# Long convolution with a gated projection on one core: the third stage multiplies with its constants held still, block by block, and its results turn through DRAM

## The chip, the cores and the metric

The kernel runs on one core of a Trainium2 chip. The metric is the device time of one execution in microseconds (us). The engines are named as the profile names them: PE (TensorE, the matmuls), PEld (PE's weight loads), DVE (VectorE), ACT (ScalarE), POOL (GpSimd) and SP (SyncE, which issues every DMA of this kernel, in order).

## The reference

Eight sequences of 6400 steps and 128 channels, all in fp32. First a causal convolution of each channel with a filter as long as the sequence, then a short gated layer:

```python
B, S, D = x.shape                      # 8, 6400, 128;  h is (6400, 128)
L = 2 * S
y = np.fft.irfft(np.fft.rfft(x, n=L, axis=1) * np.fft.rfft(h, n=L, axis=0)[None], n=L, axis=1)[:, :S, :]
...
gate_pre[t] = sum over k of conv_w[k] * y[t - 4 + k]      # 5 taps, per channel
gate = 1.0 / (1.0 + np.exp(-gate_pre))
val = y @ w_val
out = gate * val @ w_out
```

## The kernel before

The transform of 6400 points is split into 100 x 64 (`N1`, `N2`), each part a matmul with a table of constants. For one sequence ("batch") there are four stages and a gated tail:

- **Stage 1** (`first_stage`), 16 groups of 8 channels. Four matmuls a group, the data as the stationary operand (100 x 128), the table `r1` moving (200 columns). ACT or DVE copies the result in four pieces of 64x400 into `gy`, which holds one whole batch with the channel outermost: `[128, 64 channel pairs, 100 k1, 2]`.
- **Stage 2** (`second`), 13 blocks `kb` of 8 values of k1 (the last has 4). Per k1 a matmul of 128 columns with a table from `m2`, loaded per block (512 KB). `product` multiplies the block by the filter's spectrum: `swap` (ACT, two copies of 64x1024 that exchange the halves), `times_re` and `times_im` (DVE), and `summed` (POOL, for the last two blocks also DVE), which leaves the result in `gy`. The filter's two tables (`hd`, in DRAM) are loaded by `h_load` for every block, twice 512 KB, since DRAM holds each of them on all 128 rows; some were stored as one half and doubled by DRAM-to-DRAM copies (`double`).
- **Stage 3** (line 753 on), 32 groups of 4 channels. Per channel one matmul: the channel's 100 values of k1 out of `gy` are the stationary operand (128 x 100), the table `r3` moves (128 columns). So the result has k1 on the partitions, where stage 4 needs it. ACT or DVE copies each group (100x512) into `dt`. It begins when all 13 products of the batch are there, and it frees `gy`, group by group, for stage 1 of the next batch.
- **Stage 4** (line 869 on), 13 chunks of 5 time columns (the head chunk has 4). Per column two matmuls of 100 columns with `m4`, the data out of `dt` stationary.
- **The tail** of each chunk: `yc` copies it out of PSUM, the taps are added up by ACT (`first`, `q`), DVE (`more`) and POOL (`third`); then the sigmoid (ACT), the first projection ("V" below, 500 columns with `w_val`), the gate (DVE), the second projection ("P" below, 500 columns with `w_out`), a copy and the store. From the eighth chunk on (`LAGGED`) the taps of a batch wait until the next batch's stage 3.

Ahead of all that lies the head: stages 1 and 2 of the filter `h` (`spectrum` keeps its tables and stores them to `hd`) beside stages 1 and 2 of the first batch, whose product is formed straight out of PSUM (`direct`).

The order of every engine's instructions is written by a planner (`_Plan`): each step has a cost per engine and a due time from constants such as `PERIOD`, and the planner runs them forward once, choosing engine, PSUM bank and buffer. The engines then follow that order, each strictly in sequence. Stage 2 works in two of PSUM's two-bank tiles (`ps`), everything else after the head in four banks (`pb`). Line 109, which the profile shows for nearly everything, is the helper that records an instruction.

Of the kernel before, what the change touches and what calls it, by code (L numbers as in the profile page):

```python
# [16 lines left out]
C = 128  # L17
# [16 lines left out]
LATE = 35  # L34
LAGGED = 8
WHOLE = 5
STASH = 6
M2B = 4
SLOTS = 11
# [3 lines left out]
HEAD_END = 101000  # L43
PERIOD = 126600
THIRD = 44275
FOURTH = 4511
SECOND = 3959
GATE = 13466
LAGS = 9341
EARLY = 545  # L50
# [5 lines left out]
LAST = 3177  # L56
LAST_GATE = 12434
# [66 lines left out]
class _Bank:  # L124


    def __init__(self, n, wide=False):
        self.n, self.wide, self.place = n, wide, None
# [5 lines left out]
class _Slot:  # L134


    def __init__(self, head=False):
        self.users, self.head, self.place = [], head, None
# [18 lines left out]
class _Plan:  # L157
# [63 lines left out]
    def forward(self):  # L221
# [4 lines left out]
        slots = [0] * (SLOTS + 2)  # L226
        self.split = False
        port = server = now = 0
        events, began = [], []
# [11 lines left out]
        def open_slots(o):  # L241
            n = len(slots) if o.take.head else SLOTS
            return [i for i in range(n) if slots[i] is not None and slots[i] <= now]
# [19 lines left out]
        while left:  # L263
            moved = True
            while moved:
                moved = False
                for e in free:
# [20 lines left out]
                    if e == "sync":  # L288
                        server = max(now + self.LEAD, server) + dur
                        free[e] = max(free[e], server - self.LEAD - self.AHEAD)  # L290
                        o.done = server + self.LAND
                    else:
                        o.done = now + dur + self.HOP
                    if o.port and e in ("vector", "gpsimd"):
                        port = now + dur
                    if o.take is not None:
                        i = o.take.spot = min(open_slots(o), key=lambda i: (i < SLOTS, slots[i]))
                        slots[i] = None
# [6 lines left out]
                    if b is not None:  # L305
                        if o.new:
                            i, h = b.spot = self.room(b, halves, now)
                            self.split = self.split or b.n == 1 and i > 1
                            for k in (0, 1) if b.n == 2 or i < 2 else (h,):
                                halves[i][k] = None  # L310
# [40 lines left out]
    def room(self, b, halves, now):  # L351
# [3 lines left out]
        if b.n == 2:  # L355
            return next(((i, 0) for i, p in enumerate(free) if all(p) and (i < 2 or not self.split)), None)
        spot = None
        if self.split or all(all(p) for p in free[2:]):
            spot = next(((i, h) for i in (2, 3) for h in (0, 1) if free[i][h]), None)
# [33 lines left out]
def longconv_moe(ctx: ExitStack, tc: tile.TileContext, x, h, r1, m2, r3, m4, w64, out):  # L393
# [9 lines left out]
    dt = cp.tile([128, N2 * 2 * C], F32, name="dt")  # L403
    dv = dt.rearrange("p (n c d) -> p n c d", c=2, d=C)
    gh = dt[:, : N1 * C].rearrange("p (d k t) -> p d k t", k=N1, t=2)
    m4_all = cp.tile([128, N2 + 1, N1], F32, name="m4_sb")
    m4_sb = m4_all[:PX]
# [4 lines left out]
    gl = cp.tile([128, N2 - LATE, N1], F32, name="gl")  # L412
    y_sb = [cp.tile([128, XG * N2], F32, name=f"y_{i}") for i in range(YB)]
# [19 lines left out]
    def kdt(t, kb):  # L433
        n = count(kb)
        return t[:, : n * C].rearrange("p (d k t) -> p d k t", k=n, t=2)

    def spectral(bank, kb):
        n = count(kb)
        if n <= 4:
            return bank.ap()[:, 0, : n * C].rearrange("p (k d t) -> p d k t", t=2, d=C // 2)  # L440
        return bank.ap().rearrange("p b (k d t) -> p d (b k) t", t=2, d=C // 2)
# [7 lines left out]
    def cells(y, n):  # L449
        out, i = [], 0  # L450
        while i < n:
            z = y + i
            end = 4 if z < 4 else LATE if z < LATE else N2
            k = min(n - i, end - z)
            s = (z - 4) % N2
            out.append((i, gl[:, z - LATE : z - LATE + k] if z >= LATE else dv[:, s : s + k, 1, :N1]))
            i += k
        return out

    def weights():
        ti = gl.rearrange("p n t -> p (n t)")[:, : 3 * NW].bitcast(I32)
        tf = gl.rearrange("p n t -> p (n t)")[:, 3 * NW : 6 * NW]
# [43 lines left out]
        last = dma(ti[:, : 2 * NW], w64.bitcast(I32), 261)  # L508
# [74 lines left out]
    def m2_load(kb):  # L583
        k, slot, n = count(kb), _Slot(), len(m2_user)
        rows = lambda: slot.ap().rearrange("p (k c) -> p k c", c=C)[:, :k]
        op = dma(rows, m2[:, kb * KB : kb * KB + k], 64 * k, m2_user[n - M2B] if n >= M2B else [], 6000, take=slot, spare=1)
# [20 lines left out]
    def summed(kb, w, u, after, many):  # L607
# [3 lines left out]
        if kb >= NKB - many:  # L611
            where["vector"] = _dve(count(kb) * C)
        return add(
            lambda e: getattr(nc, e).tensor_tensor(out=u, in0=u, in1=kdt(w.ap(), kb), op=ADD),
            where, after, port=True, use=[w],
        )

    def times_re(kb, p, bank, hs, u, after):
        return add(
            lambda e: nc.vector.tensor_tensor(out=u, in0=spectral(bank, kb), in1=kdt(hs[0].ap(), kb), op=MUL),  # L620
            {"vector": _dve(count(kb) * C)}, [p, *after], bank=bank, use=hs[:1],
        )

    def direct(kb, p, bank, hs, re, im):
        n, w = count(kb) * C, _Slot(True)
        u = gy[:, :, kb * KB : kb * KB + count(kb)]

        def cross(e):
            t, v, hi = kdt(w.ap(), kb), spectral(bank, kb), kdt(hs[1].ap(), kb)
# [3 lines left out]
        a = times_re(kb, p, bank, hs, u, re)  # L633
        c = _times(_dve(n, held=True), 2)
        b = add(cross, {"vector": (c[0] + 120, c[1] + 30)}, [p, *im], bank=bank, take=w, use=hs[1:])
        return a, b, summed(kb, w, u, [a, b], 1)

    def product(kb, p, bank, hs, h_ready):
        n, w = count(kb) * C, _Slot()
        u = gy[:, :, kb * KB : kb * KB + count(kb)]  # L640

        def swap(e):
            t, v = kdt(w.ap(), kb), spectral(bank, kb)
            nc.scalar.activation(t[:N2], v[N2:], AF.Copy, scale=1.0 if kb < WHOLE else -1.0)
            nc.scalar.copy(t[N2:], v[:N2])

        def times_im(e):
            t = kdt(w.ap(), kb)
            nc.vector.tensor_tensor(out=t, in0=t, in1=kdt(hs[1].ap(), kb), op=MUL)
# [3 lines left out]
        a = times_re(kb, p, bank, hs, u, h_ready[:1])  # L653
        b = add(times_im, {"vector": _dve(n)}, [s, h_ready[1]], port=True, use=[hs[1], w])
        return summed(kb, w, u, [a, b], MANY)

    def h_load(kb):
        k, hs = count(kb) * C, [_Slot(), _Slot()]
# [20 lines left out]
    w_in = weights()  # L679
    stored, head_done, adds = [], [], []  # L680

    def spectrum(kb, load):
        bank, n, hs = _Bank(2), count(kb) * C, [_Slot(True), _Slot(True)]
        v = lambda: spectral(bank, kb)
        t = lambda r: kdt(hs[r].ap(), kb)
# [3 lines left out]
        r1_ = add(  # L689
            lambda e: nc.gpsimd.tensor_copy(hs[0].ap()[N2:, :n], hs[0].ap()[:N2, :n]),  # L690
            {"gpsimd": (170 + 0.86 * n,) * 2}, [r0], use=hs[:1],
        )
        i0 = add(lambda e: nc.scalar.activation(t(1)[:N2], v()[N2:], AF.Copy, scale=-1.0), cost, [p], bank=bank, take=hs[1])
        i1 = add(lambda e: nc.scalar.copy(t(1)[N2:], v()[N2:]), cost, [p], bank=bank, use=hs[1:])
        full = kb < WHOLE
        m = 2 * N2 if full else N2
        st = [dma(hd[kb, 0, :m, :n], lambda: hs[0].ap()[:m, :n], n // (2 if full else 4), [r0, *([r1_] if full else [])], use=hs[:1])]
        lo = 0 if full else N2
        st.append(dma(
            hd[kb, 1, lo:, :n], lambda: hs[1].ap()[lo:, :n], n // (2 if full else 4), [i1, *([i0] if full else [])], use=hs[1:],  # L700
        ))
        stored.append([[x] for x in st])
        return p, hs, [r0, r1_], [i0, i1], st

    for kb in range(NKB):
        plan.where = f'head {kb}'
        plan.base = 46300 + 3680 * kb
# [3 lines left out]
        plan.base += 2760  # L711
        q = second(gy, kb, stat, xs1, bank)
        a, b, c = direct(kb, q, bank, hs, re, im)
        head_done += [p, a, b, *st]
        adds.append(c)

    stashed = first_stage(x[1], stash_at, lambda g: [*firsts[: 2 * NG]], HEAD_END - 1000, 1350, range(STASH)) if B > 1 else []
# [9 lines left out]
    def double(kb, after):  # L727
        n = count(kb) * C
        lo, hi = slice(0, N2), slice(N2, 2 * N2)
        for r, (o, i) in enumerate(((hi, lo), (lo, hi))):  # L730
            stored[kb][r] = [dma(hd[kb, r, o, :n], hd[kb, r, i, :n], n // 4, [*stored[kb][r], *after])]

# [8 lines left out]
    gl_user = {}  # L741
    s4_old, dt_old, tail_old = [], head_done, {}
# [3 lines left out]

    for b in range(B):
# [308 lines left out]
```

## Time and profile before

| | before |
|---|---|
| median of 3 runs | 1047.68 us (1047.63 to 1047.81) |
| the profiled execution | 1047.48 us |
| its span, first to last instruction | 1045.7 us |
| granted clock of TensorE | 1.000 |
| moved by DMA | 221.16 MB, mean 211 GB/s |
| read from and written to DRAM | 184.47 MB and 39.32 MB |

The profile gives the busy time of each engine, the chain of work that ended last, groups of instructions with their mean duration, and the DMA issues. A matmul in fp32 stands in the trace as two records, so a count of 16 is 8 matmuls. A record's duration contains the way through the array, which the next record overlaps; what a matmul costs in a row of them is the distance from start to start.

### The profile page before, as it was taken

To read this page: it belongs to the slowest core of one execution; us is meant where nothing else is said; L and a number is where in the kernel's file an instruction comes from. 1 tells how busy PE (TensorE), PEld (TensorE's weight loads), DVE (VectorE), ACT (ScalarE), POOL (GpSimd) and SP (SyncE) were. 2 spreads that over 40 slices of the span, in tenths; PEclk is the share of its full clock that TensorE was granted. 3 is DMA by queue.
4 is the path that set the end of the run, shared out by engine and by line. 5 is a ranking of instruction groups with operands and counts; after the bars stand their busy time and mean duration, and the time that the engine had idled before them with its cause. 6 is when DMAs were issued, how large, how long until landed. Compare 5 with 4: busy or idle time off the path is not lost.

```text
span 1045.7 us, 19783 instructions
## 1 busy us (share of the span) xinstructions
PE 1037.2 (99%) x7490; PEld 937.5 (90%) x7490; DVE 752.1 (72%) x1033; ACT 794.1 (76%) x1322; POOL 347.7 (33%) x229
## 2 busy tenths in 40 slices
PE   9999999999999999999999999999999999999998
PEld 9998999889988899888998899988998889988885
DVE  6999248983699637985399745996369953898187
ACT  6688679766886869777697767878688786987675
POOL 0078106610165203731056300652027410472030
PEclk9999999999999999999999999999999999999999
DMA  9598949953399335983289633994249931691102
GB/s 267 164 351 291 357 115 327 367 195 90 118 369 365 105 92 204 370 296 91 81 287 357 230 91 90 354 356 161 87 156 377 332 95 62 237 364 42 38 31 97
DMA packets 80605, 221.16 MB, mean 211 GB/s; under 512 B 9530, under 2 KB 24990, under 8 KB 80286
## 3 DMA queue, kind: packets, MB, share of 16 engines
q1 hardware_dynamic: 80510, 219.89, 60.9%
q8 instruction: 59, 0.97, 0.4%
q14 instruction: 36, 0.29, 0.1%
HBM read 184.47 MB, written 39.32 MB: 214 GB/s over the span
## 4 chain that ended last, share of the span: by engine, by line
PE 92%; DVE 6%; issue 1%; ACT 1%; POOL 0%; DVEq 0%; POOLq 0%; ACTq 0%
PE pb L109 58%; PE ps L109 34%; DVE k L109 2%; DVE gy L109 2%; DVE dt L109 1%; DVE gl L109 0%; POOL gy L109 0%; ACT k L109 0%; ACT m_sb L109 0%; ACT dt L109 0%; ACT y_head L109 0%; ACT y L109 0%; DVE q L109 0%; DVEq L109 0%; POOLq L109 0%
## 5 line engine op out<-in xcount | busy, mean ns | idle before, releaser
L109 ACT COPY gy<-ps 64x400 f32<-64x400 f32 x452 | 219.6, 486 | 86.2 <-PE ps L109 81.8
L109 PEld LDWEIGHTS pb<-r_sb,gy 128*100 128x100 f32 x2016 | 236.5, 171 | 26.0 <-issue 24.0
L109 PEld LDWEIGHTS pb<-m_sb,dt 100*128 100x128 f32 x1988 | 232.6, 192 | 24.7 <-issue 13.7
L109 PE MATMUL pb<-r_sb,gy 128*100 128x128 f32 x2016 | 242.8, 273 | 0.0
L109 PE MATMUL pb<-m_sb,dt 100*128 100x100 f32 x1988 | 235.5, 274 | 0.0
L109 POOL TENSOR_TENSOR gy<-gy,k 128x1024 f32<-128x1024 f32 x89 | 211.4, 2379 | 69.7 <-PE pb L109 38.1
L109 PEld LDWEIGHTS ps<-gy,k 128*128 128x128 f32 x1600 | 195.1, 188 | 23.0 <-issue 17.6
L109 PE MATMUL ps<-gy,k 128*128 128x128 f32 x1600 | 201.3, 278 | 0.4 <-ACT k L109 0.4
L109 DVE COPY dt<-pb 100x512 f32<-100x512 f32 x145 | 100.1, 691 | 133.1 <-PE pb L109 130.6
L109 PE MATMUL ps<-r_sb,x 100*128 100x200 f32 x976 | 184.1, 333 | 1.6 <-DVE k L109 0.8
L109 PEld LDWEIGHTS ps<-r_sb,x 100*128 100x128 f32 x976 | 162.4, 190 | 8.6 <-issue 4.8
L109 DVE SCALAR_TENSOR_TENSOR dt<-pb,w_sb,dt 128x500 f32<-128x500 f32 (+7 forms) x210 | 127.7, 624 | 5.4 <-ACT q L109 1.5
L109 ACT ACTIVATE k<-ps 64x1024 f32<-64x1024 f32 (+1 forms) x101 | 99.7, 987 | 36.7 <-PE ps L109 33.7
L109 DVE TENSOR_TENSOR k<-k,k 128x1024 f32<-128x1024 f32 (+1 forms) x91 | 124.5, 1374 | 0.0
L109 DVE TENSOR_TENSOR gy<-ps,k 128x1024 f32<-128x1024 f32 (+1 forms) x96 | 113.2, 1180 | 11.9 <-ACT k L109 9.3
L109 ACT COPY k<-ps 64x1024 f32<-64x1024 f32 (+2 forms) x109 | 104.7, 961 | 5.2 <-PE ps L109 2.6
L109 DVE SCALAR_TENSOR_TENSOR gl<-y,w_sb,gl 128x500 f32<-128x500 f32 (+3 forms) x122 | 85.6, 708 | 31.2 <-POOL gl L109 29.4
L109 POOL TENSOR_TENSOR dt<-dt,q 128x500 f32<-128x500 f32 (+1 forms) x64 | 66.2, 1036 | 107.9 <-ACT k L109 43.5
L109 POOL TENSOR_TENSOR gl<-gl,q 128x500 f32<-128x500 f32 (+1 forms) x45 | 52.7, 1172 | 141.1 <-DVE gl L109 132.6
L109 POOL MEMSET dt<- 128x4 f32 x8 | 0.8, 104 | 291.5 <-PE pb L109 291.5
L109 ACT COPY y<-pb 128x500 f32<-128x500 f32 (+1 forms) x126 | 71.2, 565 | 32.0 <-PE pb L109 25.3
L109 ACT COPY dt<-pb 100x512 f32<-100x512 f32 x107 | 61.6, 586 | 34.7 <-PE pb L109 34.0
(69 smaller groups left out, 934.5 us busy)
## 6 DMA issues: line engine op xcount, KB each, us to landing
k<-hd SPq DMA_DIRECT2D x168, 512.0 KB, 5.8
k<-m SPq DMA_DIRECT2D x96, 512.0 KB, 5.9
x<-xl SPq DMA_DIRECT2D x114, 224.0 KB, 2.6
out<-y SPq DMA_DIRECT2D x84, 250.0 KB, 3.8
hd<-hd SPq DMA_DIRECT2D x14, 256.0 KB, 5.9
k<-hd SPq DMA_DIRECT2D x14, 256.0 KB, 4.5
hd<-k SPq DMA_DIRECT2D x6, 512.0 KB, 6.5
out<-k SPq DMA_DIRECT2D x11, 250.0 KB, 2.3
```

The lines of the kernel that those rows point to most:

```text
L109: r = self._tc.keep_in_program_order(call(*args, **kwargs))
```

## The change

- **Stage 3** (`third`) now follows each product block. The table `r3` is the stationary operand and the block moves, 4 values of k1 times 128 channels, 512 columns a matmul: 25 matmuls a batch in place of 128. The result has (n2, real or imaginary) on the partitions and k1 along the row.
- **The turn.** ACT or DVE copies each 128x512 result to a buffer; when a block is complete, a store writes it to DRAM (`zd`, one of two) as `[k1][n2, c][channel]`: pieces of 512 bytes, 1024 of them a block. Per chunk of stage 4 a load fetches its columns with k1 on the partitions (112 rows of 5 KB). Five chunk buffers (`RING`).
- **The filter's tables** are kept in DRAM as one half each. `h_load` loads 64 rows (256 KB) and POOL copies them to the other 64 partitions (`twice`). The doubling in DRAM is gone.
- **Buffers.** Products are in slots of their own, no longer in `gy`, with k1 outermost, so that every product instruction reads and writes one straight row. 17 slots in place of 11. Stage 1 of the next batch waits for stage 2's matmuls alone. The gate's values are in one row (`ga`), so the second projection isn't split where they lay in two places. The taps no longer lag, but for the last batch.
- **The planner's** constants are new, and it now lets SP have 8 DMAs outstanding. The weights and `m4` are loaded later, behind the first batch's input.

```diff
+    def third(kb, b, summed_, u):
+        n, to, done = count(kb), _Slot(), []
+        for q in range(0, n, 4):
+            bank = _Bank(1, head=b == 0)
+            def mm(e, q=q, bank=bank):
+                nc.tensor.matmul(bank.ap(), lhsT=r3_sb, rhs=u.ap()[:, q * C : (q + 4) * C], start=True, stop=True)
+            def ev(e, q=q, bank=bank):
+                copiers[e](to.ap()[:, q * C : (q + 4) * C], bank.ap())
+            p = add(mm, {"tensor": _pe(855, 1)}, [summed_, r3_in], bank=bank, new=True, use=[u])
...
+            done.append(add(ev, {"scalar": _act(512), "vector": _dve(512)}, [p], bank=bank, **more))
+        o = zd[b % 2][kb * KB : kb * KB + n, : 2 * N2].rearrange("k p d -> p k d")
+        return dma(o, lambda: to.ap()[:, : n * C].rearrange("p (k d) -> p k d", d=C), 76 * n, done, use=[to])
+    def twice(slot, n, after):
+        return add(
+            lambda e: nc.gpsimd.tensor_copy(slot.ap()[N2:, :n], slot.ap()[:N2, :n]),
+            {"gpsimd": (170 + 0.86 * n,) * 2}, after, port=True, use=[slot],
+        )
     def h_load(kb):
...
-            ops.append(dma(
-                lambda slot=slot: slot.ap()[:, :k], hd[kb, r, :, :k], k // 2, [*head_done, *stored[kb][r]], 6000,
-                take=slot, spare=1,
-            ))
+            i = dma(
+                lambda slot=slot: slot.ap()[:N2, :n], hd[kb, r, :, :n], n // 4, [stored[kb][r]], 6000,
+                take=slot, spare=SPARE,
+            )
+            ops.append(twice(slot, n, [i]))
...
-        for q in range(C // 4):
-            bank = _Bank(1, not nxt or b == 0)
-            def mm(e, q=q, bank=bank):
-                for i in range(4):
-                    d = 4 * q + i
-                    nc.tensor.matmul(
-                        bank.ap()[:N1, i * 2 * N2 : (i + 1) * 2 * N2],
-                        lhsT=gy[:, d // 2, :, d % 2],
-                        rhs=r3_sb,
...
+            before = list(passed)
+            ys1 = first_stage(x[b + 1], gy_at, lambda g: before, begin, FIRST)
...
+                p = second(gy, kb, stat, ys1, bank)
+                passed.append(p)
+                way(b + 1, kb, product(kb, p, bank, hs, h_ready[:1], h_ready[1:], -1.0, MANY))
...
+            z_in = dma(
+                zt[:PX, : 2 * n * C].rearrange("p (n d) -> p n d", d=C), zd[b % 2][:, 2 * a : 2 * (a + n)],
+                PX * n, [*back, *z_old, rows[b % 2]], 5000,
+            )
...
-                            lhsT=dv[:N1, a + q, c, :],
+                            lhsT=v[:N1, q, c, :],
...
-            p = add(mm, {"tensor": _pe(448, n)}, [*s3e, *(m4_in if b == 0 else [])], bank=bank, new=True)
+            p = add(mm, {"tensor": _pe(448, n)}, [z_in, *(m4_in if b == 0 else [])], bank=bank, new=True)
```

On PE, in the middle of the program before, stage 3 (the rows with `r_sb` and `gy`) stands in a stretch of its own, mixed with stage 1 of the next batch (`r_sb` and `x`), and stages 4 and 2 follow:

```order
L109 MATMUL ps_95<-r_sb,x_90 128x200 x4
L109 MATMUL pb_853<-r_sb,gy 100x128 x4
L109 MATMUL ps_94<-r_sb,x_91 128x200 x4
L109 MATMUL pb_853<-m_sb,dt 128x100 x8
L109 MATMUL pb_854<-m_sb,dt 128x100 x10
L109 MATMUL ps_94<-gy,k_87 128x128 x8
L109 MATMUL ps_95<-gy,k_81 128x128 x8
L109 MATMUL pb_853<-m_sb,dt 128x100 x10
```

In the changed program the same stretch of PE, where stage 2 of a batch begins (rows with `gy` are stage 2, rows with `k` and `r_sb` the new stage 3, `w_sb` the projections):

```order
L114 MATMUL ps_94<-gy,k_81 128x128 x8
L114 MATMUL ps_95<-gy,k_87 128x128 x8
L114 MATMUL pb_97<-dt,w_sb 128x500
L114 MATMUL pb_1026<-y_all,w_sb 128x500
L114 MATMUL pb_97<-m_sb,dt 128x100 x10
L114 MATMUL ps_94<-gy,k_78 128x128 x8
L114 MATMUL pb_1026<-dt,w_sb 128x500
L114 MATMUL pb_1027<-k_81,r_sb 128x512
L114 MATMUL ps_95<-gy,k_83 128x128 x8
L114 MATMUL pb_1026<-k_81,r_sb 128x512
L114 MATMUL pb_1027<-k_73,r_sb 128x512
```

Stage 3 has moved from a stretch of its own to places some seven rows behind the stage 2 of its block (that of the first row here begins in the eighth), in single matmuls of 512 columns.

At the last batch PE of the changed program has, between its last matmul of stage 3 (`k_86`) and its first chunk of stage 4 (the last row), one chunk of the batch before and nine projections:

```order
L114 MATMUL pb_96<-k_86,r_sb 128x512
L114 MATMUL pb_97<-m_sb,dt 128x100 x10
L114 MATMUL pb_96<-dt,w_sb 128x500
L114 MATMUL pb_1027<-y_all,w_sb 128x500
L114 MATMUL pb_96<-y_all,w_sb 128x500
L114 MATMUL pb_1026<-dt,w_sb 128x500
L114 MATMUL pb_96<-dt,w_sb 128x500
L114 MATMUL pb_96<-y_all,w_sb 128x500
L114 MATMUL pb_97<-y_head,w_sb 128x400
L114 MATMUL pb_96<-dt,w_sb 128x500
L114 MATMUL pb_97<-dt,w_sb 128x400
L114 MATMUL pb_1026<-m_sb,dt 128x100 x8
```

Before, the evictions of a batch's stage 3 ran group by group beside its matmuls, and the first chunk followed at once. In the other batches nine groups of stage 1 stand in this stretch of the changed program as well.

On SP of the changed program, at the end of a batch, the store of the last block is followed by loads of the next batch's input, and then by the chunk loads, which wait for all 13 stores of the batch:

```order
L114 DMA zd_103<-k_78 128x4x128
L114 DMA x_90<-xl 112x512
L114 DMA out<-y_all 128x500
L114 DMA k_71<-hd 64x1024
L114 DMA x_91<-xl 112x512
L114 DMA x_88<-xl 112x512
L114 DMA dt<-zd_103 112x1024
L114 DMA dt<-zd_103 112x1280 x2
```

Before, SP had neither the `zd` stores nor the `dt` loads, and stage 4 read `dt` as the evictions had left it.

More of the change, by code (lines that the diff above doesn't have):

```diff
@@ L42 @@
 YB = 6
[L43 to L50, printed above, removed]
+HEADS = 46300
+HEAD_STEP = 5140
+HEAD_END = 119306
+PERIOD = 115119
+WEIGHTS = 60000
+M4 = 60000
+ROWS = 90000
+FIRST = 2513
+SECOND_AT = 41901
+SECOND = 4969
+EARLY = 12753
+FOURTH = 8959
+GATE = 23743
 PATIENCE = 380
@@ L124, with __init__ @@
 class _Bank:
-    def __init__(self, n, wide=False):
-        self.n, self.wide, self.place = n, wide, None
+    def __init__(self, n, wide=False, head=False):
+        self.n, self.wide, self.head, self.place = n, wide, head, None
     def ap(self):
@@ L241, in open_slots @@
         def open_slots(o):
-            n = len(slots) if o.take.head else SLOTS
-            return [i for i in range(n) if slots[i] is not None and slots[i] <= now]
+            return [i for i in range(SLOTS) if slots[i] is not None and slots[i] <= now]
         def fits(o, e):
@@ L355, in room @@
         if b.n == 2:
[L356 to L359, printed above, removed]
+            return next(((i, 0) for i, p in enumerate(free[:2 if self.split else 3]) if all(p)), None)
+        spot = next(((3, h) for h in (0, 1) if free[3][h]), None)
+        if spot is None and not b.head and (self.split or all(free[2])):
+            spot = next(((2, h) for h in (0, 1) if free[2][h]), None)
         if spot is None and b.wide:
@@ L447, in dma, with weights @@
         return add(run, {"sync": _dma(kb)}, after, early=early, **more)
[L449 to L464, printed above, removed]
+    def weights(after):
+        ti = y_all[:, : 3 * NW].bitcast(I32)
+        tf = y_all[:, 3 * NW : 6 * NW]
         w = ti[:, : 2 * NW].rearrange("p (n two) -> p two n", two=2)
@@ L612, in summed, with run @@
             where["vector"] = _dve(count(kb) * C)
-        return add(
[L614 to L621, printed above, removed]
+        def run(e):
+            o = flat(u.ap(), kb)
+            getattr(nc, e).tensor_tensor(out=o, in0=o, in1=flat(w.ap(), kb), op=ADD)
@@ L622, in times_re @@
+        return add(run, where, after, port=True, use=[w, u])
+    def times_re(kb, p, bank, hs, u, after, held=False):
+        return add(
+            lambda e: nc.vector.tensor_tensor(out=flat(u.ap(), kb), in0=spectral(bank, kb), in1=flat(hs[0].ap(), kb), op=MUL),
+            {"vector": _dve(count(kb) * C, held=held)}, [p, *after], bank=bank, take=u, use=hs[:1],
         )
     def direct(kb, p, bank, hs, re, im):
-        n, w = count(kb) * C, _Slot(True)
-        u = gy[:, :, kb * KB : kb * KB + count(kb)]
+        n, w, u = count(kb) * C, _Slot(), _Slot()
@@ L636, in direct, with product @@
[L636 to L640, printed above, removed]
+        b = add(cross, {"vector": (c[0] + 70, c[1] + 30)}, [p, *im], bank=bank, take=w, use=hs[1:])
+        return summed(kb, w, u, [a, b], 1), u
+    def product(kb, p, bank, hs, re, im, scale, many):
+        n, w, u = count(kb) * C, _Slot(), _Slot()
         def swap(e):
[L643 to L644 removed]
+            t, v = flat(w.ap(), kb), spectral(bank, kb)
+            nc.scalar.activation(t[:N2], v[N2:], AF.Copy, scale=scale)
@@ L710, in longconv_moe @@
         bank = _Bank(2)
-        plan.base += 2760
+        plan.base = HEADS + HEAD_STEP * kb + 2760
         q = second(gy, kb, stat, xs1, bank)
[L713 to L717, printed above, removed]
+        passed.append(q)
+        if kb not in SWAPPED:
+            pre = direct(kb, q, bank, hs, re, im)
+        else:
+            pre = product(kb, q, bank, hs, re, im, 1.0, 1)
+        way(0, kb, pre)
     m4_in = []
```

262 lines of the change are left out of this document (109 added, 153 removed).

## The prediction

> **What bounds the kernel now.** I read the page's busy times and chain first. Columns: busy us, share of the span, instructions; then the share of the last chain by engine.
>
> ```profile
> PE 1037.2 (99%) x7490; PEld 937.5 (90%) x7490; DVE 752.1 (72%) x1033; ACT 794.1 (76%) x1322; POOL 347.7 (33%) x229
> PE 92%; DVE 6%; issue 1%; ACT 1%; POOL 0%; DVEq 0%; POOLq 0%; ACTq 0%
> ```
>
> PE is never free and carries the chain. What its work costs I read from starts in two stretches of PE's timeline (start us, length us, then operation and count of records, two to a matmul).
>
> ```profile
> 235.82 1.52 PE L109 MATMUL ps<-r_sb,x 100*128 100x200 f32 x8
> 237.18 1.00 PE L109 MATMUL pb<-y,w_sb 128*128 128x500 f32 x2
> 238.02 1.91 PE L109 MATMUL pb<-r_sb,gy 128*100 128x128 f32 x16
> 239.76 1.00 PE L109 MATMUL pb<-gl,w_sb 128*128 128x500 f32 x2
> ...
> 286.12 2.04 PE L109 MATMUL ps<-gy,k 128*128 128x128 f32 x16
> 287.99 2.37 PE L109 MATMUL pb<-m_sb,dt 100*128 100x100 f32 x20
> 290.20 2.04 PE L109 MATMUL ps<-gy,k 128*128 128x128 f32 x16
> 292.08 1.00 PE L109 MATMUL pb<-y,w_sb 128*128 128x500 f32 x2
> 292.92 2.37 PE L109 MATMUL pb<-m_sb,dt 100*128 100x100 f32 x20
> 295.13 1.06 PE L109 MATMUL pb<-dt,w_sb 128*128 128x400 f32 x4
> 296.02 2.03 PE L109 MATMUL ps<-gy,k 128*128 128x128 f32 x16
> ```
>
> From start to start: a stage 1 group takes 1.36 us, a projection of 500 columns 0.84, eight third-stage matmuls of 128 columns 1.74 (0.2175 each), a block of stage 2 1.87, a chunk of stage 4 2.21. A batch on PE is then 16 x 1.36 = 21.8, 12.5 x 1.87 = 23.4, 128 x 0.2175 = 27.8, 64/5 x 2.21 = 28.3, and 24 projections and two of 400 columns, 21.5: 122.8 us. Eight batches and the filter's 45.2 make 1028 of the span's 1045.7. So what leaves PE leaves the time, as long as nothing else comes to stand there.
>
> The windows view shows where (window: length, busy of PE, PEld, DVE, ACT, POOL, granted clock, DMA share, GB/s): two stretches of the head, one between stages 3 and 1, one of stage 2.
>
> ```profile
> 62.00:74.00 12.00, 12.00 (x106) 12.00 (x106) 11.69 (x11) 9.94 (x11) 10.67 (x8) 1.00 1.02 399
> 84.00:100.00 16.00, 14.13 (x111) 13.42 (x109) 15.63 (x13) 12.60 (x16) 14.11 (x9) 1.00 0.91 281
> 262.00:274.00 12.00, 12.00 (x95) 12.00 (x93) 4.55 (x7) 8.22 (x18) 0.00 (x0) 1.00 0.30 86
> 288.00:330.00 42.00, 42.00 (x306) 36.28 (x305) 40.25 (x48) 34.86 (x48) 28.45 (x17) 1.00 1.00 367
> ```
>
> In stage 2 the DMAs are as full as PE (share 1.00 at 367 GB/s); elsewhere they are at 0.3. That is the second limit, and the change adds to it.
>
> **The change, part by part.** The profiled execution took 1047.48 us, 0.2 under the median of the runs; I sum against it.
>
> *Stage 3 on PE.* A matmul of 512 columns isn't in the trace; by the 500-column rows it takes 0.84 x 512/500 = 0.86 us, whatever stands still. 25 of them are 21.5 us a batch in place of 27.8: 6.34 less, times eight, **-50.7**. Once less per batch the projection split in two (295.13 to 296.02, 0.89 in place of 0.84): **-0.4**. A batch on PE is 116.5 us.
>
> *The head.* Between 84 and 100 us PE works 14.13 of 16, since DVE is full. Now each block brings PE 1.7 us of third stage as well, which fills that: **-1.9**.
>
> *Evictions and POOL.* The rows (busy us, mean ns):
>
> ```profile
> L109 DVE COPY dt<-pb 100x512 f32<-100x512 f32 x145 | 100.1, 691 | 133.1 <-PE pb L109 130.6 <-ACT gy L109 0.3
> L109 ACT COPY dt<-pb 100x512 f32<-100x512 f32 x107 | 61.6, 586 | 34.7 <-PE pb L109 34.0 <-DVE gl L109 0.3
> L109 POOL COPY dt<-dt 64x1024 f32<-64x1024 f32 x7 | 7.2, 1032 | 51.6 <-ACT dt L109 51.2
> L109 POOL TENSOR_TENSOR gy<-gy,k 128x1024 f32<-128x1024 f32 x89 | 211.4, 2379 | 69.7 <-PE pb L109 38.1 <-DVE k L109 28.2 <-DMA k<-hd 1.3
> L109 DVE TENSOR_TENSOR k<-k,k 128x1024 f32<-128x1024 f32 x84 | 120.2, 1431 | 0.0
> L109 ACT COPY k<-ps 64x1024 f32<-64x1024 f32 x98 | 98.4, 1004 | 3.7 <-POOL gy L109 1.3 <-PE ps L109 1.1
> ```
>
> 25 evictions a batch in place of 32, off the path: 0, with 36 us less for DVE and ACT together; PE covers them, and without cover seven would cost 4.5 us a batch. POOL gets 26 copies of at most 1.03 us for the filter's halves, some 180 us in all: 530 of a thousand, not a bound. But they stand in one queue with `summed` and the taps, and PE's third stage waits for `summed`: rival 2.
>
> *The DMAs.* The issues (count, KB each, median us to landing):
>
> ```profile
> k<-hd SPq DMA_DIRECT2D x168, 512.0 KB, 5.8
> k<-m SPq DMA_DIRECT2D x96, 512.0 KB, 5.9
> x<-xl SPq DMA_DIRECT2D x114, 224.0 KB, 2.6
> out<-y SPq DMA_DIRECT2D x84, 250.0 KB, 3.8
> hd<-k SPq DMA_DIRECT2D x8, 256.0 KB, 4.9
> out<-k SPq DMA_DIRECT2D x11, 250.0 KB, 2.3
> ```
>
> Per batch now: `m2` 6400 KB, filter halves 6400 (12800 before), input 3584, output 3200, chunk loads 12 x 560 + 448 = 7168, `zd` stores 6400. At 367 GB/s 6400 KB take 17.9 us.
>
> The halves need not run at that rate. From 62 to 74 us, with full-height stores, the DMAs move 399 GB/s at share 1.02; from 84 to 100, with half-height stores of 64 rows for about half of the bytes, 281 at 0.91, or 309 for a full share against 391. So a half moves at about 1/(2/309 - 1/391) = 255 GB/s: 25.7 us a batch, not 17.9. [...]
>
> The stores' 512-byte pieces, 12,800 a batch over 16 engines, are in no row. Below: as fast per byte as all else, 17.9 us, 22 ns a piece. Above: the 262 to 274 window moves packets of 2 KB at 0.30 and 86 GB/s, so 16 x 0.30 x 2048/86 = 114 ns each; in 288 to 330 one of 4 KB takes 16 x 4096/367 = 179; the straight line through both gives 66 ns for 512 bytes, 53 us a batch. I take 22 us (27 ns), near the lower end: the first window is hardly loaded, so its packets contain waiting that a full queue hides. [...]
>
> In all 17.9 + 25.7 + 10.0 + 8.9 + 20.0 + 22 = 104.5 us of DMA in 116.5. The load is uneven. From a batch's first stage 2 to its last third stage PE has 23.4 + 21.5, seven chunks (15.5) and 16 projections (13.4), 73.8 us; the DMAs have 17.9 + 25.7 + 22, four chunk loads (6.2) and four outputs (2.8), 74.6. Two or three blocks are loaded ahead, which softens it. I take **+2** a batch, 14 in seven, between 0 and 6. The head is tighter: 68 us of PE in stages 2 and 3 against 17.9 + 25.7 (the filter's half-height stores) + 22 + 8 of `m4` + some 8 of reloads, 82; the stores may trail, the `m2` loads may not: **+6**, 0 to 14. SP issues in order: each `zd` store waits for its second eviction, each first chunk load for all 13 stores, and behind both stand the loads of the next blocks or input; that is in the same terms.
>
> *The turn at a batch's end.* Last third stage, eviction 0.6 to 0.7, store 2.3 to 4.9, chunk load 2.6 to 5.8: 5.5 to 11.4 us. Nine groups of stage 1 (12.2) and the projections cover it. At the last batch there are only a chunk and nine projections, 2.2 + 7.2 = 9.4: **+2**, 0 to 6.
>
> Sum: 1047.5 - 50.7 - 0.4 - 1.9 + 14 + 6 + 2 = **1016.5 us**.
>
> **Rivals.**
>
> 1. *The 512-byte pieces bind: slower.* By the stage 2 stretch the DMAs without them take 52.6 of 73.8 us, so from 26 ns a piece PE begins to wait; with 6.4 us more a batch (35 ns, or 51 if the whole batch's slack can be used) the gain is gone. At 66 ns a batch takes 82.5 + 53 = 135 us, and the whole about 996 + 8 x 19 = 1146. For it: DMA already at 1.00 in stage 2. Against: 379 to 399 GB/s never needed more than large packets to be full, and the straight line rests on idle queues. Price 1030 to 1146; 0.25, of which 0.15 slower by over 0.2%, 0.03 within, 0.07 still faster.
> 2. *PE waits for the product.* From a block's stage 2 to its third stage: two ACT copies (2.0), `times_im` (1.43), `summed` on POOL (2.38), 5.8 us, against 8.5 us of other rows on PE (1.87 + 0.84 + 0.84 + 2.21 + 1.87 + 0.84). A POOL copy (1.03) and a tap ahead of `summed` eat 2.3 of the 2.7 left. 0.3 us at each of 12 blocks and 7 batches is 25 us on top of what the DMAs take: 1018 to 1040. For: POOL's and DVE's loads grow. Against: in 288 to 330 the same chain ran beside a full PE. 0.08, all faster.
> 3. *All is hidden.* Prefetch carries the stretch: 994 to 1003. 0.15.
> 4. *A wide matmul costs less than its width.* [...] The 0.84 of 500 columns stands against it: 3.9 times the 0.2175 of 128, as its width is. [...] 0.01.
>
> **How the numbers follow.** The forecast, 1003 to 1030, has 0.50. Faster by over 0.2% (2.1 us, about what a measurement of this kernel can tell): 0.50 + 0.07 + 0.08 + 0.15 + 0.01 = 0.81; within: 0.03; slower: 0.15 of rival 1 and 0.01 left for an order that jams: 0.16. The range leaves out the worse two thirds of rival 1 (0.17) and the low end of rival 3 (0.03): 997 to 1045. The predicted time is the forecast's, 1016.
>
> **What would show it.** Third-stage matmuls 0.86 us apart; DMA share near 1.0 from stage 2 on and about 0.7 elsewhere; PE's few waits at stage 2 for `m` and `hd` loads and at the start of stage 1. Wrong: a `zd` store that lands long after 5 us, PE waiting for POOL at stage 3, or a full DMA share throughout.

## The result, and the profile after

The changed kernel is slower. Four runs gave 1104.43 us median (1098.41 to 1108.14), the kernel before beside it 1047.66 (1047.46 to 1047.81): a ratio of 1.054, 95% interval 1.049 to 1.059. Forecast were 1016 us and a range of 997 to 1045. The profiled execution took 1102.85 us, its span is 1101.0, TensorE's mean granted clock 0.961.

The page of the changed kernel: busy times, the granted clock in 40 slices, the DMAs' share, the main DMA queue (packets, MB, share of 16 engines), the chain by engine and by line, and five kinds of DMA with their size and their median time to landing.

```profile
PE 1034.5 (94%) x5826; PEld 816.4 (74%) x5826; DVE 820.4 (75%) x1072; ACT 713.8 (65%) x1163; POOL 525.6 (48%) x389
PEclk9999979999999899989899899998999999998999
DMA  9698999999889897999979999899989999698582
...
q1 hardware_dynamic: 185182, 280.22, 92.2%
...
PE 58%; DMA 28%; DVE 8%; issue 2%; ACT 2%; POOL 1%; SPq 1%; DVEq 0%; POOLq 0%; ACTq 0%
...
dt<-zd SPq DMA_DIRECT2D x95, 560.0 KB, 8.2
k<-m SPq DMA_DIRECT2D x96, 512.0 KB, 7.2
zd<-k SPq DMA_DIRECT2D x96, 512.0 KB, 6.3
k<-hd SPq DMA_DIRECT2D x168, 256.0 KB, 7.8
x<-xl SPq DMA_DIRECT2D x116, 224.0 KB, 7.2
```

The chain was 92% PE; now 28% of it is DMA, and the DMA row is near full up to its last slices. The filter's tables, half the bytes of before, take longer to land: 7.8 us for 256 KB, where 512 KB took 5.8. The input's loads went from 2.6 to 7.2. How full the DMAs are, and at what rate, one window over the steady part says for each kernel (us, length, busy of PE, PEld, DVE, ACT, POOL, granted clock, DMA share, GB/s). Before:

```profile
300.00:900.00 600.00, 600.00 (x4346) 540.94 (x4344) 424.94 (x574) 466.47 (x786) 195.86 (x126) 1.00 0.61 212
```

and the changed kernel (the second row, a stretch of 30 us, is used further down):

```profile
300.00:900.00 600.00, 565.52 (x3161) 439.43 (x3160) 449.14 (x569) 391.30 (x629) 320.12 (x234) 0.96 0.96 261
...
470.00:500.00 30.00, 25.64 (x123) 18.18 (x122) 18.01 (x20) 14.57 (x21) 17.70 (x13) 0.83 0.99 264
```

A share of 0.61 at 212 GB/s is 348 GB/s for full DMAs; 0.96 at 261 is 272. (The share adds up the times of the packets and can pass 1: it is 1.04 in e6_whole below; "full" is a measure to compare by, not a limit.) The DMAs did not only get more to do, each byte also takes 28% longer. A batch's 33,152 KB, 33.95 MB, need 33.95/0.2719 = 124.9 us of full DMAs, where the prediction had 104.5, and PE needs 116.5. So DMA is the longer of the two: at a share of 0.96 a batch takes 124.9/0.96 = 130.1 us in place of 116.5. With 53.0 us less of PE's work, and the head's batch counted like the other seven, that is 1047.5 - 53.0 + 8 x 13.6 = 1103 us, against 1102.85. Rate and share are this run's own, so the sum only shows where the time is, about the same in every batch; it doesn't say why.

Where PE feels it, the chain between 470 and 497 us shows (start, length, what):

```profile
469.02 4.29 PE pb L114 x10
...
474.09 11.63 DMA zd<-k
...
485.81 0.70 DVE k L114
486.52 0.04 issue
486.56 9.52 PE pb L114 x26
```

and the same moment in the timeline (start, length, operation, and the idle time ahead of it with what ended it):

```profile
471.41 1.88 PE L114 MATMUL pb<-k,r_sb 128*128 128x512 f32 x4
...
473.13 2.46 PE L114 MATMUL pb<-m_sb,dt 100*128 100x100 f32 x20
...
485.81 0.69 DVE L114 COPY k<-pb 128x512 f32<-128x512 f32 x1 [6.00 <-DMA zd<-k]
485.82 0.59 ACT L114 COPY k<-pb 128x512 f32<-128x512 f32 x1 [6.30 <-DMA zd<-k]
...
486.56 4.59 PE L114 MATMUL pb<-m_sb,dt 100*128 100x100 f32 x20 [4.18 <-DVE k L114]
```

A store of third-stage results is issued at 474.09, just behind four loads of tables (469.08 to 472.80 on SP), and lands 11.6 us later. Its buffer is the one that the next evictions write, so DVE and ACT stand for 6 us, and PE for 4.2. Then comes a second loss that no part of the prediction had: the next ten matmuls (20 records) take 4.59 us, where ten of the same kind took 2.46 at 473.13. Between 470 and 500 us the granted clock is 0.83, and while those ten matmuls run it is 0.50:

```profile
486.50:491.20 4.70, 4.64 (x21) 4.64 (x22) 4.14 (x6) 1.97 (x3) 0.41 (x1) 0.50 1.06 302
```

The timeline above also gives the new third stage its price: from 471.41 to 473.13 there are 1.72 us for two matmuls of 512 columns, 0.86 each.

The waits add up alike (engine, line, what it waited for: us in total, times, longest):

```profile
POOL k L114 <- DMA k<-hd: 148.4, 30, 16.6
...
ACT k L114 <- DMA zd<-k: 45.2, 9, 7.4
DVE k L114 <- DMA zd<-k: 39.2, 7, 7.1
...
PE pb L114 <- DVE k L114: 22.4, 6, 4.2
PE ps L114 <- DMA x<-xl: 19.9, 10, 3.2
```

POOL waits for the filter's halves, the evictions wait for stores, PE for evictions and for input. In these rows it is DMA that comes late, of every kind. The question is why the DMAs move 272 GB/s when full, and no longer 348.

### The profile page after: what moved, and what is told of

Read it like the earlier page. It is cut to its first block, busy times and chain, and to the rows that moved or that the text cites. A ratio compares the mean times of both kernels' runs of the same rounds, so it can differ in the third digit from the quotient of the medians.

```text
span 1101.0 us, 17151 instructions
## 1 busy us (share of the span) xinstructions
PE 1034.5 (94%) x5826; PEld 816.4 (74%) x5826; DVE 820.4 (75%) x1072; ACT 713.8 (65%) x1163; POOL 525.6 (48%) x389
## 3 DMA queue, kind: packets, MB, share of 16 engines
HBM read 194.98 MB, written 86.79 MB: 256 GB/s over the span
## 4 chain that ended last, share of the span: by engine, by line
PE 58%; DMA 28%; DVE 8%; issue 2%; ACT 2%; POOL 1%; SPq 1%; DVEq 0%; POOLq 0%; ACTq 0%
PE pb L114 35%; PE ps L114 24%; DMA zd<-k 9%; DMA k<-hd 7%; DMA x<-xl 5%; DVE k L114 4%; DVE dt L114 3%; DMA dt<-zd 3%; DMA out<-y_head 1%; DVE y_all L114 1%; ACT k L114 1%; DMA k<-m 1%; POOL dt L114 1%; DMA out<-y_all 1%; DVE gy L114 1%
## 5 line engine op out<-in xcount | busy, mean ns | idle before, releaser
L114 POOL COPY k<-k 64x1024 f32<-64x1024 f32 (+1 forms) x195 | 199.1, 1038 | 262.1 <-DMA k<-hd 144.3
L114 PE MATMUL pb<-m_sb,dt 100*128 100x100 f32 x2008 | 252.9, 285 | 24.8 <-DVE k L114 22.4
L114 DVE SCALAR_TENSOR_TENSOR dt<-pb,w_sb,dt 128x500 f32<-128x500 f32 (+7 forms) x328 | 221.4, 685 | 37.2 <-POOL dt L114 11.9
L114 POOL TENSOR_TENSOR k<-k,k 128x1024 f32<-128x1024 f32 x89 | 210.5, 2365 | 67.7 <-DVE k L114 25.6
L114 POOL TENSOR_TENSOR dt<-dt,q 128x500 f32<-128x500 f32 x93 | 115.8, 1245 | 214.5 <-DVE dt L114 118.4
L114 PE MATMUL pb<-k,r_sb 128*128 128x512 f32 x400 | 200.0, 622 | 0.8 <-POOL k L114 0.8
L114 DVE COPY gy<-ps 64x400 f32<-64x400 f32 x200 | 114.3, 572 | 106.3 <-PE ps L114 104.1
L114 DVE TENSOR_TENSOR k<-ps,k 128x1024 f32<-128x1024 f32 (+1 forms) x130 | 152.3, 1177 | 24.5 <-PE ps L114 13.6
L114 ACT COPY y_all<-pb 128x500 f32<-128x500 f32 x139 | 79.8, 574 | 95.2 <-PE pb L114 82.3
L114 PEld LDWEIGHTS pb<-k,r_sb 128*128 128x128 f32 x400 | 73.9, 199 | 69.8 <-issue 47.1
L114 PE MATMUL pb<-dt,w_sb 128*128 128x500 f32 (+2 forms) x206 | 103.0, 596 | 1.6 <-DVE dt L114 1.5
```

Of the source, the lines that this page charges most:

```text
L114: r = self._tc.keep_in_program_order(call(*args, **kwargs))
```

## The experiments

Three theories. **P, the partitions:** how fast a transfer moves depends on which of the 128 partitions of SBUF it touches. The change makes the filter's loads touch half of them (0 to 63), and its chunk loads are of 112 rows as the input is. **S, the stores:** 12,800 pieces of 512 bytes a batch slow down everything beside them. **C, the mix:** DRAM is now written 86.79 MB in place of 39.32, and reading and writing disturb each other. In every number below, "DMA us a batch" is a batch's bytes over the rate at full share, worked out from the window 300 to 900 us as above.

### The halves on other partitions (e2_half32, g3_top64)

```diff
-                lambda slot=slot: slot.ap()[:N2, :n], hd[kb, r, :, :n], n // 4, [stored[kb][r]], 6000,
+                lambda slot=slot: slot.ap()[32:96, :n], hd[kb, r, :, :n], n // 4, [stored[kb][r]], 6000,
```

In g3_top64 `slot.ap()[N2:, :n]` stands there. Order, bytes and packets are the same in both. The products then read rows of the tables in which other numbers lie, in both runs; one turns out fast and one slow, so it isn't the numbers that decide.

> The halves of the filter's tables are loaded to partitions 32 to 95 in place of 0 to 63, same bytes, same order; POOL still copies the lower half up, so the products are of other numbers. [...] Theories S and C: no change, 1098 to 1108 us.

> The changed kernel with the halves of h loaded to partitions 64 to 127 in place of 0 to 63; order and bytes are the same, the tables' lower rows keep old values, so the numbers are wrong. If what counts is how many partition groups a transfer spans over a fixed pattern that repeats in the upper half, this is as slow as 0 to 63: 1090 to 1115 us. If 32 to 95 was fast only because the lowest partitions are left (they take other traffic, or the copy to the other half reads them), it is fast as well: 1020 to 1050 us.

Measured: 1024.9 us on partitions 32 to 95 (ratio to before 0.977, 0.973 to 0.981), and 1119.8 on 64 to 127 (1.067, 1.062 to 1.072). The windows, first of e2_half32, then of g3_top64:

```profile
300.00:900.00 600.00, 596.48 (x3489) 469.48 (x3488) 490.91 (x638) 432.74 (x706) 349.67 (x257) 1.00 0.94 288
```

```profile
300.00:900.00 600.00, 557.14 (x3110) 435.07 (x3109) 439.25 (x560) 386.08 (x620) 314.24 (x228) 0.95 0.96 256
```

The loads of the halves in the two runs, e2_half32 first:

```profile
k<-hd SPq DMA_DIRECT2D x168, 256.0 KB, 5.9
```

```profile
k<-hd SPq DMA_DIRECT2D x168, 256.0 KB, 8.3
```

One slice in one line takes 80 us away, where S and C had no change at all: 288 GB/s at 0.94 is 306 full, 111 us a batch, 14 less than the changed kernel. PE is busy 596 of 600 us again, at full clock. The upper 64 partitions are no better than the lower 64 (1120 us, 5 more than its slow case had), so it isn't something that lies at partition 0. It is the set that counts, not its size, which is 64 rows in all three: 1104 us on 0 to 63 and 1120 on 64 to 127, against 1025 on 32 to 95. Why the set matters, no run here shows.

### 128 rows in place of 112 (e1_px128, g5_chunk128, e5_both)

```diff
-PX = 112
+PX = 128
```

In e1_px128 this makes input, fourth-stage constants and chunk loads 128 rows high (14% more bytes each), in the changed kernel's order. g5_chunk128 does it for the chunk loads alone. e5_both is e1_px128 with e2_half32, and so has its misplaced tables.

> The chunk loads, the input and m4 go to 128 partitions in place of 112 (28 rows of padding), the order of all engines as in the changed kernel. [...] Theory S (the 512-byte stores slow everything) and theory C (reads and writes of DRAM together are simply slow): 14% more bytes in 11 MB a batch, about 4 us more: about 1130 us.

> The changed kernel with chunk loads of 128 rows (640 KB) as in e1_px128, but input and fourth-stage constants left at 112 rows; same order, same result. If the 112 rows of the chunk loads cost what e1_px128 gained, it has most of the 34 us: 1065 to 1085 us. If the gain came from the input's loads, which stage 1 waits for, it stays at 1095 to 1110. By bytes alone (14% more per chunk load, about 1 us a batch at 367 GB/s more for 1.0 MB, 2.8 us) it would be slower: 1105 to 1130.

> Both of the edits that moved transfers to other partitions at once (128 partitions for input, chunk loads and m4; the filter's halves to partitions 32 to 95, so the products are of other numbers), order as in the changed kernel. Theory P: DMA share under 0.85, PE binds, 975 us of matmuls by their rows and some 25 of head, end and small waits: 1000 us, granted clock above 0.99. If the two gains were one and the same (any slack helps once): no better than 1025 us.

Measured: e1_px128 1070.4 us (ratio 1.021, 1.016 to 1.026), g5_chunk128 1080.2 (1.029, 1.026 to 1.031), e5_both 1008.5 (0.962, 0.961 to 0.963). The windows of e1_px128 and of e5_both:

```profile
300.00:900.00 600.00, 575.16 (x3242) 448.42 (x3241) 463.33 (x596) 403.77 (x659) 332.29 (x246) 0.97 0.96 286
```

```profile
300.00:900.00 600.00, 600.00 (x3539) 475.39 (x3539) 500.66 (x645) 437.80 (x715) 351.98 (x259) 1.00 0.91 305
```

More bytes took less time, where S and C had expected 1130 us. 34,688 KB a batch at 298 GB/s are 119 us, 6 less than 33,152 KB took. Of the 34 us that e1_px128 gains on the changed kernel, about 24 are the chunk loads'. Both edits together give 335 GB/s full and 106 us a batch, and PE is busy through the whole window. That is 40 us faster than before, of the 53 that the change takes off PE. The expectation had 1000 us and a share under 0.85; the 1025 of its rival, that the two gains are one and the same, is excluded.

The price of 112 rows can be seen without halves and stores beside it. From 2 to 30 us every one of these kernels loads `x` and `h` into SBUF with full DMAs. First the kernel before, with 112 rows, then e1_px128, with 128:

```profile
2.00:30.00 28.00, 28.00 (x156) 26.89 (x156) 20.48 (x39) 17.52 (x37) 0.00 (x0) 1.00 1.03 288
```

```profile
2.00:30.00 28.00, 28.00 (x150) 26.95 (x150) 18.30 (x32) 16.85 (x36) 0.00 (x0) 1.00 0.99 348
```

That is 280 GB/s full against 352. Brought to a full share in the same way, all runs with 112 rows in these loads have 250 to 280 GB/s in this stretch, and all with 128 rows 336 to 361. Why 112 rows are slower than 128, no run here shows.

### The pieces of 512 bytes, and the chunk loads' bytes (e3_zd4k, e4_znarrow)

```diff
-        o = zd[b % 2][kb * KB : kb * KB + n, : 2 * N2].rearrange("k p d -> p k d")
-        return dma(o, lambda: to.ap()[:, : n * C].rearrange("p (k d) -> p k d", d=C), 76 * n, done, use=[to])
+        o = zd[b % 2][kb * KB : kb * KB + n].rearrange("k p d -> (k p d)")[: 2 * N2 * n * C].rearrange("(p x) -> p x", p=2 * N2)
+        return dma(o, lambda: to.ap()[:, : n * C], 76 * n, done, use=[to])
```

In e3_zd4k the stores write the same bytes in rows of 4 KB, so the results lie in DRAM in another order than the chunk loads read. In e4_znarrow a chunk load fetches one column of five:

```diff
-                zt[:PX, : 2 * n * C].rearrange("p (n d) -> p n d", d=C), zd[b % 2][:, 2 * a : 2 * (a + n)],
+                zt[:PX, : 2 * C].rearrange("p (n d) -> p n d", d=C), zd[b % 2][:, 2 * a : 2 * (a + 1)],
```

> The turn's stores write the same bytes in pieces of 4 KB, one per partition, so the blocks stand in DRAM in another order and stage 4 gets other numbers; all else as in the changed kernel. Theory P: their own packets cost 16 us a batch in place of 23, 7 us less, about 1050 us, and the loads keep their long packets. Theory S: the loads' packets fall back as well (4 KB from 245 ns to about 165, 5 KB from 310 to about 200), 20 us less or more, PE binds again: 1000 to 1010 us. Theory C: 1050 us, as P.

> Each chunk load fetches one time column in place of five, 80% fewer bytes, the rest of stage 4's operands is left as it lies; same order, same waits. All theories that put the time on the DMAs: 20 us or more less a batch, PE binds, 990 to 1015 us, granted clock 1.0. If instead PE waits for the chain of the product on ACT, DVE and POOL (rival 2 of the prediction): above 1070 us.

Measured: e3_zd4k 1084.8 us (1.037, 1.032 to 1.041), e4_znarrow 1025.4 (0.980, 0.975 to 0.986), some 10 us above what I had written. Their windows, e3_zd4k first:

```profile
300.00:900.00 600.00, 575.76 (x3226) 446.71 (x3225) 458.03 (x586) 401.24 (x649) 331.54 (x245) 0.97 0.94 268
```

```profile
300.00:900.00 600.00, 594.81 (x3466) 466.89 (x3465) 486.86 (x634) 429.23 (x700) 346.76 (x254) 1.00 0.86 237
```

e3_zd4k met no expectation: S had 1000 to 1010 us, P and C 1050. With 4 KB pieces the DMAs still need 119 us a batch, more than PE's 116.5, and at a share of 0.94 a batch takes 127: the small pieces cost about 6 us a batch, and S is not the cause. Four fifths of the chunk loads are worth 124.9 - 102 = 23 us a batch (27,440 KB at 276 GB/s), so all of them an estimated 28.6, where the prediction had 20.0.

### Whole tables (e6_whole, g1_whole128)

```diff
-    hd = dp.tile([NKB, 2, N2, KB * C], F32, name="hd")
+    hd = dp.tile([NKB, 2, 2 * N2, KB * C], F32, name="hd")
...
-                lambda slot=slot: slot.ap()[:N2, :n], hd[kb, r, :, :n], n // 4, [stored[kb][r]], 6000,
+                lambda slot=slot: slot.ap()[:, :n], hd[kb, r, :, :n], n // 2, [stored[kb][r]], 6000,
...
-            ops.append(twice(slot, n, [i]))
```

The filter's tables lie in DRAM on 128 rows again, and POOL's copies in the blocks of seven batches are gone. The planner makes its own order of it. g1_whole128 has 128 rows for input and chunk loads as well; its order differs a little from e6_whole's, since the planner's costs follow the rows.

> The filter's tables are kept and loaded whole again (128 rows, 512 KB, no POOL copies), the rest of the change stays; the planner orders anew. [...] A rival that puts the loss on the POOL copies in front of the products: faster than 1090 us.

> e6_whole with 128 rows in place of 112 for input, chunk loads and fourth-stage constants. In e6_whole the main DMA queue was busy 99.3% of 1086.3 us, 1079 us: its DMAs are the only limit. From the changed kernel to e1_px128 the same queue's time fell from 92.2% of 1101.0 to 91.2% of 1065.5, by 43 us. So by the theory of the partitions the queue's time is 1079 - 43 = 1036 us, still the limit, and with the head and the end the time is 1040 to 1055 us. If e6_whole was slow for another reason than its DMA time (its other order, the longer loads in front of the products), 128 rows give less than 15 us: above 1070.

Measured: e6_whole 1085.8 us (1.036, 1.034 to 1.038), g1_whole128 1024.8 (0.977, 0.976 to 0.979). The windows, e6_whole first:

```profile
300.00:900.00 600.00, 557.85 (x3201) 434.81 (x3199) 447.65 (x600) 389.42 (x620) 200.32 (x116) 0.97 1.04 322
```

```profile
300.00:900.00 600.00, 597.47 (x3488) 468.52 (x3488) 478.95 (x653) 429.93 (x695) 213.46 (x126) 1.00 1.01 358
```

and the queue with two of its loads, in e6_whole and in g1_whole128:

```profile
q1 hardware_dynamic: 198494, 332.65, 99.3%
...
k<-hd SPq DMA_DIRECT2D x168, 512.0 KB, 8.0
dt<-zd SPq DMA_DIRECT2D x95, 560.0 KB, 10.2
```

```profile
q1 hardware_dynamic: 202766, 348.31, 97.0%
...
k<-hd SPq DMA_DIRECT2D x168, 512.0 KB, 7.3
dt<-zd SPq DMA_DIRECT2D x95, 640.0 KB, 6.9
```

e6_whole lies in the interval of the rival, the copies in front of the products; g1_whole128 came out faster than the 1040 to 1055 us of theory P. e6_whole moves 52 MB more than the changed kernel and is 19 us faster. A batch needs 40.5 MB at 310 GB/s, 131 us against 125, so the bytes did cost 6 us. (A whole table lands after 8.0 us, a half on 0 to 63 after 7.8.) The gain lies elsewhere: the DMAs are kept busier, a share of 1.04 for 0.96, or 131/1.04 = 126 us a batch against 130. POOL's 190 us of copies are gone (the page has POOL at 31% for 48%) and the order is new; this run doesn't tell the two apart. That the copies are not what makes the changed kernel slow, e2_half32 shows: it has all of them, in the same order, at 1025 us.

With 128 rows the program moves 349 MB in place of 334 and takes 61 us less: 42.1 MB at 354 GB/s, 119 us. I had expected the queue's time to fall by 43 us, as from the changed kernel to e1_px128; it fell from 1079 to 97.0% of 1021.8 = 991, by 88. In these two pairs 112 rows cost more where the queue was fuller. The result speaks against C as well: g1_whole128 has the most bytes of all runs, writes more to DRAM than the changed kernel (95.48 MB against 86.79), and has the highest rate.

### The half clock (e7_warm)

```diff
-                p = second(gy, kb, stat, ys1, bank)
+                p = second(gy, kb, stat, ys1, bank, 16 if kb == 10 else 0)
```

Stage 2 of one block a batch repeats its last matmul 16 times, with the same result, to shorten PE's idle time at the place where the chain waits.

> In every batch but the first, block 10 of stage 2 repeats its last matmul 16 times (3.7 us of PE, same result), just ahead of the place where PE waited 4 us and then ran at half its clock; order unchanged. [...] If the half clock is itself what costs the time after each wait: up to 4.5 us in each of seven batches, 1070 to 1080 us.

Measured: 1098.9 us (1.044, 1.037 to 1.051), 6 to 10 us under the changed kernel by medians or ratios, with intervals that overlap. The window:

```profile
300.00:900.00 600.00, 577.28 (x3353) 452.71 (x3353) 458.77 (x580) 399.32 (x643) 332.32 (x241) 0.99 0.98 265
```

The clock in the steady part rises from 0.96 to 0.99, over the whole span from 0.961 to 0.983. That is 0.017 x 1094 = 19 us of clock lost in place of 0.039 x 1101 = 43. Had the half clock set the time, these 24 us should have shown, and at most 10 did: the DMAs are at 0.98. In the changed kernel the half clock came behind waits: at 357.18, 486.56 and 619.12 us ten matmuls took 4.59 us each time, at a granted clock of 0.50, after PE had stood for 3.55, 4.18 and 4.07 us. That it costs a few us of its own isn't excluded.

### Kernels that keep the halves and the result (f1_turned128, g4_oneload)

Both compute the reference, with input and chunk loads of 128 rows. f1_turned128 loads the halves to partitions 32 to 95 and fills the rest with two copies of 32 rows on POOL or ACT:

```diff
-                lambda slot=slot: slot.ap()[:N2, :n], hd[kb, r, :, :n], n // 4, [stored[kb][r]], 6000,
+                lambda slot=slot: slot.ap()[32:96, :n], hd[kb, r, :, :n], n // 4, [stored[kb][r]], 6000,
...
-            ops.append(twice(slot, n, [i]))
+            ops.append([turned(slot, n, [i], 32, 96), turned(slot, n, [i], 64, 0)])
```

g4_oneload brings both halves in one load of 128 rows and makes the two tables with three copies of 64 rows:

```diff
+        c1 = moved(lambda: u.ap()[:N2], lambda: t.ap()[N2:], [i], use=[t, u])
+        c2 = moved(lambda: u.ap()[N2:], lambda: t.ap()[N2:], [i], use=[t, u])
+        c3 = moved(lambda: t.ap()[N2:], lambda: t.ap()[:N2], [c1, c2], use=[t])
```

> The two edits as a kernel of right numbers: halves stored with their rows turned, loaded to partitions 32 to 95, and completed by two copies of 32 rows each on POOL or ACT (52 copies a batch in place of 26, each about 1 us); input, chunk loads and m4 on 128 partitions; the planner orders anew. Theory P: 1000 to 1015 us. [...]

> A kernel that computes the reference: both halves of h come in one load of 128 rows (real parts in the lower, imaginary in the upper 64), three copies of 64 rows on POOL or ACT make the two tables of it, and input and chunk loads have 128 rows. No transfer of the steady state touches fewer than 100 partitions. By the theory of the partitions the DMA queue has about the time of e5_both, 88% of 1005 us, and PE is the limit again: 1005 to 1025 us, of which up to 12 us for one copy per block more than in the changed kernel (f1_turned128 with two more lost 24 us against e5_both). If the copies hold the products back instead, 1032 us or more.

Measured: f1_turned128 1032.2 us (0.985, 0.984 to 0.987), g4_oneload 1030.9 (0.984, 0.981 to 0.986). The group of copies in the changed kernel (busy us, mean ns, idle ahead of them),

```profile
L114 POOL COPY k<-k 64x1024 f32<-64x1024 f32 x180 | 190.8, 1074 | 253.7 <-DMA k<-hd 144.3 <-ACT k L114 58.7 <-DVE k L114 34.7
```

and those in f1_turned128, with its window:

```profile
L114 POOL COPY k<-k 32x1024 f32<-32x1024 f32 x179 | 184.8, 1042 | 175.4 <-DMA k<-hd 111.4 <-DVE k L114 39.2 <-issue 14.5
L114 ACT COPY k<-k 32x1024 f32<-32x1024 f32 x157 | 162.2, 1042 | 4.4 <-DMA k<-hd 1.5
...
300.00:900.00 600.00, 592.67 (x3445) 462.17 (x3444) 467.22 (x628) 545.54 (x818) 340.68 (x256) 1.00 0.89 296
```

A copy of 32 rows takes 1.04 us, as long as one of 64 in the changed kernel (1.07), so the copy of each table costs twice. The DMAs are relieved (0.89 at 296 GB/s, 107 us a batch), but 24 us of e5_both's gain go to the copies and to the new order that the planner makes around them. f1_turned128 so landed above the 1000 to 1015 us of theory P. g4_oneload, with three copies to a block in place of four, lies between its two intervals and gains nothing sure on that, and both lie behind g1_whole128, which copies nothing in the steady blocks. The fastest kernel with the right result is g1_whole128, 2.3% faster than before: the third stage as changed, the filter's tables whole, and input and chunk loads on all 128 partitions.

## Why the prediction was wrong, point by point

The packets that the traces record, by size, price the terms of the prediction's sum one by one. Mean ns of a packet between 300 and 900 us:

| packets | before | changed | e2_half32 | e6_whole | g1_whole128 |
|---|---|---|---|---|---|
| 512 bytes: the turn's stores | | 29 | 28 | 28 | 28 |
| 2000 bytes: output, 128 rows | 86 | 93 | 87 | 88 | 85 |
| 2048 bytes: input, 112 rows (128 in g1_whole128) | 116 | 118 | 110 | 112 | 96 |
| 4096 bytes: the filter's tables and `m2` | 178 | 252 | 199 | 192 | 176 |
| 5120 bytes: chunk loads, 112 rows (128 in g1_whole128) | | 312 | 295 | 321 | 217 |

(Before, most input packets took 84 ns, and a few of 361 raise the mean.) In the order of the rows, a batch of the changed kernel has 12,800, some 1640, 1792, 3200 and 1344 of them, and 112 of 4 KB for the head chunk. Over 16 engines that is 22.9 us for the stores, 9.5 for the output, 13.2 for the input, 50.4 for halves and `m2`, and 28.0 for the chunk loads: 124 us. The prediction had 22, 8.9, 10.0, 43.6 and 20.0: 104.5.

- *Stage 3 on PE, -50.7.* Right: 0.86 us a matmul, 400 records. e5_both shows most of the gain, 40 us, once the DMAs are out of the way. There PE's busy time is 48.8 us less than before, and PE stands 8 us longer, nearly all of it in the head: 10.6 of the first 150 us in place of 3.4, and 5.8 in place of 4.3 at the end. So the third stage's work did not fill the head's gaps (the term of -1.9), while +6 for the head and +2 for the end were about right in that run.
- *What bounds the kernel, and that the DMAs come next.* Right in kind. The prediction left the DMAs the second limit, with 104.5 us in 116.5. They are the first, with 124.9. In e5_both, with halves on 32 to 95 and 128 rows in the other loads, the DMAs need 106, and the time, 1008.5 us, falls into the forecast.
- *Chunk loads 20.0, input 10.0 at 367 GB/s.* **The step that failed**, with the next one. The rate was that of loads of 128 rows, and it was put on loads of 112. The chunk loads take 28.0 us by their packets (28.6 by e4_znarrow), the input 13.2. The trace of before had the price, in a stretch that the prediction did not read: the 2 to 30 us shown under e1_px128, 280 GB/s full. At that rate the chunk loads come to 26 us and the input to 13.
- *The halves, 25.7 us.* Mis-sized in the same way. Partitions 32 to 95 in place of 0 to 63 take 14 us off a batch. If halves on 32 to 95 run at the 367 GB/s of the prediction, 17.9 us, those on 0 to 63 take an estimated 32, or 205 GB/s; the packets of 4 KB give as much, 50.4 less 17.8 for `m2` at the 178 ns of before. The 255 GB/s came from stores of half height in a stretch of the head, and was put on loads; why it was too high stays open.
- *The stores, 22 us.* Right: 29 ns a piece, 22.9 us. Rival 1, the one priced case that could end slower, named the wrong mechanism; that its price from the point where DMAs become the limit, 1030 to 1146, contains the result is luck.
- *+2 a batch.* Its working rested on full DMAs that catch up outside of stage 2. With 124.9 us against 116.5 nothing is left to catch up in; it became 13.6 a batch.
- *Rival 2, PE waits for the product.* Seen in another form: PE did wait for DVE and ACT, 22.4 us in the largest row, but they waited for stores.
- The text's own signs of failure were a store that lands long after 5 us and a full DMA share throughout, and the trace shows both.

## What to carry to other kernels

In these runs a DMA rate held only for the partitions of the transfers that it was read from: before halving a load's rows, ask which partitions remain, since half the rows on partitions 0 to 63 saved little here and on 32 to 95 much more (with `m2`, 50 and 40 us of DMA time a batch, where whole tables took 53 to 58). When a second resource is within some 10% of the first after a change, its terms have to be priced as carefully as the gain, and at the load that they will run under. A kernel whose DMAs are full may be helped by moving more bytes, if they go to other partitions: g1_whole128 moves 349 MB, with input and chunk loads on 128 partitions, and takes 61 us less than e6_whole, which moves 334 with them on 112.

## What the runs showed of the hardware

- The same 64-row loads of 256 KB: the kernel takes 1104 us with them on partitions 0 to 63, 1120 on 64 to 127, 1025 on 32 to 95; the loads land in 7.8, 8.3 and 5.9 us.
- Loads of 128 rows with 14% more bytes landed sooner than those of 112, at a DMA share of 1.01 and 1.04: 6.9 us for 640 KB in g1_whole128 against 10.2 for 560 KB in e6_whole; a packet of 5 KB took 217 ns there against 321.
- Stores to DRAM in pieces of 512 bytes took 28 to 29 ns a piece in the runs of the table, beside 85 to 93 ns for the output's pieces of 2000 bytes, some 20 to 30% more time for a byte.
- A COPY of rows of 1024 numbers took about as long for 32 rows as for 64: 1.04 us for 32x1024 in f1_turned128, 1.07 for 64x1024 in the changed kernel, both on POOL.
- After PE stood for 4.2 us, ten matmuls took 4.59 us in place of 2.46, and the granted clock was 0.50 while they ran.
